# A two-way branch turned round, its target announced ahead, and the first tile's work put in another order

## The chip, the cores and the metric

The kernel runs on one core of one Trainium2 chip, in one launch. The metric is the device time of that launch in microseconds (us). The engines of a core run their own instruction streams side by side and wait for each other by semaphores: TensorE (PE, with its weight loads shown as PEld), VectorE (DVE), ScalarE (ACT), GpSimd (POOL) and SyncE (SP), which here mostly issues DMA transfers. A "q" behind an engine's name (ACTq, SPq) is its sequencer: register loads, branches, semaphore instructions and DMA issues.

## What is computed

Three stages follow each other, all in 32-bit floats, for a batch of 4 sequences of 576 tokens. The core of the reference:

```python
# 1. top-32 attention, 8 heads of 64
scores = scale * np.matmul(q, k.transpose(0, 1, 3, 2))
kth = np.partition(scores, -top_k, axis=-1)[..., -top_k:-top_k + 1]
scores = np.where(scores >= kth, scores, -1000000000.0)
attn = np.exp(scores - np.max(scores, axis=-1, keepdims=True))
attn = attn / (np.sum(attn, axis=-1, keepdims=True) + 1e-09)
x = np.matmul(attn, v)                    # -> (4, 576, 512)
# 2. one of 8 experts a token; a token whose gate is >= 0.5 keeps the expert of the token before it
fresh_e = int(np.argmax(logits[b, s]))
e = fresh_e if s == 0 or local_gate[b, s] < 0.5 else (prev_e if prev_e >= 0 else fresh_e)
p = np.exp(ls); p /= p.sum() + 1e-09      # ls: logits less their maximum
out[b, s] = p[e] * (np.maximum(x[b, s] @ w1[e], 0.0) @ w2[e])
# 3. Fourier mix over tokens and features, norm, two dense layers
mixed = np.real(np.fft.fft(np.fft.fft(x, axis=1), axis=2))
u = x + mixed
un = (u - mu) / np.sqrt(var + 1e-06)
out = u + np.maximum(un @ w_ch1, 0.0) @ w_ch2
```

## The kernel before

**Attention** works on 16 pairs of heads, 9 tiles of 128 query rows each, 144 tiles in all, in a software pipeline written out in one loop over `n`: the string `ORDER` says in which order the steps of a turn are issued, `OFF` how many tiles each step runs ahead or behind. A tile passes through four matmuls of its scores (`scores`, L452) into PSUM `acc`, their copy to SBUF `ss` (`evac_s`, ACT, L459), eight MAX8 on DVE (L465), and from there to the 32nd largest value, the mask, the softmax and the product with V. Ahead of the loop `prep_first` (L387 to L404) makes the operands of the first pair: `turn` transposes `in_k` and `in_q` on PE into `tp` (L358, and L359 for the last 64 rows); ACT and DVE then write a high part and a low part of each, for k (`kt`, L396 and L397), a copy of them to the other half of the partitions (L403, L404), and for q (`qp`, L401 and L402, 512 columns and then 64). It does so for head `s=0` and then for `s=1`, and `scores(0)` and `evac_s(0)` are issued behind all of it, though tile 0 needs head 0 alone.

**Routing** (`tokens`) runs a batch at a time. For the last batch it is a chain of small DVE, PE and ACT operations that ends in `slow_i` (L762, whether some expert has more tokens than its capacity or the fast top-32 failed) and in the copy of the token's numbers into `xtok` (L765). Five indirect DMAs on POOL (L780), each followed by a small memset (`spacer`, L786), write the batch's tokens to `xs_d` in DRAM, each at its expert's slot.

**The branch** (L1064, L1065) comes next: every engine loads `slow_i` into a register, compares, and either runs the body (exact attention again, and the tokens over an expert's capacity) or skips it. With these inputs it is skipped. The body lies in the instruction streams between the branch and what follows.

**The experts** follow. The first expert's first layer has been computed ahead of the branch for the slots that earlier batches fill (`early_layers`, PE, L605, into `acc`). Behind the branch PE transposes more tokens (L1207), ACT and DVE make the high and low parts `hh` (L1260) and `hl` (L1261) of that layer's result, and PE multiplies them with the second weights (L1281, into `m`). SP reads the index of the first expert (L1072), loads the slots that the last batch has filled (`load_slots`, `xsl<-xs_d`, L1182 and L1184; they are transposed later, at L1207 again, and multiplied at L1256), and at `j == 8` the indices of the other seven (L1379). `j` counts steps of an expert's 8 slices, `r` the experts and `f` the slices. Three tables of the Fourier stage are loaded on POOL's queue at `j == 10` and `j == 18` (L1385 to L1388).

The instructions of each engine lie in DRAM and are brought to it by DMA while it runs, in the packets of the two queues that the profile lists with the kind "instruction".

## Time and profile before

| | |
|---|---|
| median of 3 runs (lowest, highest) | 1240.64 us (1239.56, 1242.19) |
| the profiled execution | 1238.55 us |
| its span, first to last instruction | 1236.8 us |
| PE busy | 1187.6 us, 96% |
| DVE, ACT, POOL busy | 865.4, 679.0, 442.5 us |
| mean granted clock of PE | 0.987 of full speed |
| instruction DMA: q8 and q14 | 71 packets, 1.16 MB; 68 packets, 0.56 MB |

The times below count from the first instruction of the profiled execution. Attention fills the first 490 us, the experts come up to about 750 us, the Fourier mix and the dense layers take the rest. The median lies 2.09 us above the profiled execution's own time.

### The profile page before, as it was taken

To read this page: it belongs to the slowest core of one execution; us is meant where nothing else is said; L and a number is where in the kernel's file an instruction comes from. 1 tells how busy PE (TensorE), PEld (TensorE's weight loads), DVE (VectorE), ACT (ScalarE), POOL (GpSimd) and SP (SyncE) were. 2 spreads that over 40 slices of the span, in tenths; PEclk is the share of its full clock that TensorE was granted. 3 is DMA by queue.
4 is the path that set the end of the run, shared out by engine and by line. 5 is a ranking of instruction groups with operands and counts; after the bars stand their busy time and mean duration, and the time that the engine had idled before them with its cause. 6 is when DMAs were issued, how large, how long until landed. Compare 5 with 4: busy or idle time off the path is not lost.

```text
span 1236.8 us, 25334 instructions
## 1 busy us (share of the span) xinstructions
PE 1187.6 (96%) x8721; PEld 1084.6 (88%) x8721; DVE 865.4 (70%) x3598; ACT 679.0 (55%) x1440; POOL 442.5 (36%) x566
## 2 busy tenths in 40 slices
PE   6999999999999997899999999989999999999998
PEld 5999898998998996798888888979999999999997
DVE  7999899999999995476676785667744444543222
ACT  6999999999999894254445453533322222221111
POOL 3667686886777596000111112025410000000221
PEclk9999999999999998899999998999999999999999
DMA  5766635443543232686666675943310110100111
GB/s 112 209 169 193 149 81 116 127 103 84 142 101 88 69 126 99 202 265 235 209 224 209 228 254 152 243 146 125 122 50 34 35 66 6 67 1 1 52 52 52
DMA packets 124904, 154.43 MB, mean 125 GB/s; under 512 B 68007, under 2 KB 70303, under 8 KB 124668
## 3 DMA queue, kind: packets, MB, share of 16 engines
q1 hardware_dynamic: 119421, 134.81, 38.2%
q0 software_dynamic: 5200, 17.64, 4.3%
q8 instruction: 71, 1.16, 0.4%
q14 instruction: 68, 0.56, 0.1%
q10 hardware_dynamic: 144, 0.26, 0.1%
HBM read 93.03 MB, written 33.99 MB: 103 GB/s over the span
## 4 chain that ended last, share of the span: by engine, by line
PE 36%; issue 17%; POOL 2%; DVE 2%; DMA 2%; ACT 1%; another core or an unknown queue 1%; SPq 0%; POOLq 0%; ACTq 0%; DVEq 0%
PE f L1650 16%; PE f L1670 16%; POOL xf_d L961 2%; PE p L1151 1%; PE m L1539 1%; DMA raw<-xf_d 1%; PE acc L1546 1%; PE lt L1509 1%; DMA ut<-xf_d 0%; DVE wlo L230 0%; DMA xf_d<-xe,sid 0%; DVE raw L1130 0%; PE acc L1281 0%; PE m L1256 0%
## 5 line engine op out<-in xcount | busy, mean ns | idle before, releaser
L491 POOL TENSOR_TENSOR y<-ss,g 128x576 f32<-128x576 f32 x144 | 184.9, 1284 | 117.1 <-ACT g L486 66.3
L465 DVE MAX8 cd<-ss 128x8 f32<-128x72 f32 x1152 | 218.7, 221 | 9.8 <-ACT ss L459 9.1
L1654 ACT ACTIVATE fhh<-f 128x256 fp32r<-128x256 f32 x144 | 55.1, 383 | 275.9 <-PE f L1650 275.9
L1655 DVE SCALAR_TENSOR_TENSOR fhl<-f,fhh 128x256 fp32r<-128x256 f32 x144 | 61.0, 424 | 204.1 <-ACT fhh L1654 203.9
L562 PE MATMUL u<-in_v,et 128*128 128x74 f32 (+1 forms) x1600 | 184.7, 264 | 4.6 <-DVE dv L713 2.5
L562 PEld LDWEIGHTS u<-in_v,et 128*128 128x128 f32 (+1 forms) x1600 | 176.8, 181 | 9.5 <-ACT st_x L569 3.3
L545 PE MATMUL tp<-ident,z 128*128 128x128 f32 x720 | 143.4, 285 | 4.5 <-DVE lo L372 3.8
L546 PE MATMUL tp<-huge_id,bb 128*128 128x128 bf16 x720 | 132.4, 221 | 0.4 <-ACT bb L524 0.4
L452 PE MATMUL acc<-kt,qp 128*128 128x288 f32 x640 | 125.4, 324 | 6.3 <-ACT ss L459 4.0
L1681 POOL DMA_INDIRECT out_dram<-ut,orow x16 | 15.4, 963 | 308.3 <-DVE ut L1675 306.5
L486 ACT ACTIVATE g<-ss,mt 128x576 bf16<-128x576 f32 x144 | 118.3, 822 | 5.4 <-DVE mt L479 5.3
L545 PEld LDWEIGHTS tp<-ident,z 128*128 128x128 f32 x720 | 107.0, 149 | 15.4 <-POOL z L533 3.2
L524 ACT ACTIVATE bb<-ss,kth 128x576 bf16<-128x576 f32 x144 | 117.4, 815 | 0.0
L496 DVE MAX8 y<-y 128x8 f32<-128x576 f32 x144 | 107.2, 744 | 5.9 <-POOL y L491 5.9
L533 POOL TENSOR_SCALAR z<-ss,mt 128x576 f32<-128x576 f32 x144 | 108.4, 753 | 3.4 <-PE tp L546 3.4
L551 ACT ACTIVATE et<-tp 128x640 f32<-128x640 f32 x144 | 106.8, 742 | 3.5 <-PE tp L546 3.0
L961 POOL DMA_INDIRECT xf_d<-xe,sid x23 | 26.8, 1165 | 229.0 <-DVE xe L958 227.0
L459 ACT ACTIVATE ss<-acc 128x576 f32<-128x576 f32 x144 | 100.0, 694 | 12.0 <-PE acc L452 8.2
L452 PEld LDWEIGHTS acc<-kt,qp 128*128 128x128 f32 x640 | 94.5, 198 | 9.7 <-ACT ss L459 5.0
L1650 PEld LDWEIGHTS f<-nxh,whi 128*128 128x128 f32 x576 | 87.8, 188 | 14.0 <-ACT dd L1551 2.0
L230 DVE TENSOR_TENSOR wlo<-raw,whi 128x1024 fp32r<-128x1024 f32 x70 | 85.4, 1256 | 12.3 <-ACT whi L228 12.3
L1650 PE MATMUL f<-nxh,whi 128*128 128x256 f32 x576 | 91.3, 280 | 1.9 <-ACT dd L1551 1.7
(313 smaller groups left out, 2747.1 us busy)
## 6 DMA issues: line engine op xcount, KB each, us to landing
raw<-in_moe_w_dram SPq DMA_DIRECT2D x32, 1024.0 KB
kt<-hi SPq DMA_DIRECT2D x60, 144.0 KB
kt<-lo SPq DMA_DIRECT2D x60, 144.0 KB
xs_d<-xtok SPq DMA_DIRECT2D x8, 1056.0 KB
fr<-in_moe_w_ch_dram SPq DMA_DIRECT2D x16, 512.0 KB
raw<-in_moe_w_ch_dram SPq DMA_DIRECT2D x16, 512.0 KB
md<-md_d SPq DMA_DIRECT2D x9, 516.0 KB
in_k<-in_k_dram SPq DMA_DIRECT2D x32, 128.0 KB
```

Source lines behind the costliest of these rows:

```text
L452: PE.matmul(p, QP[i][:, s, o:o + 128].bitcast(F32R), KT[i][j][:, s, c].bitcast(F32R), start=(s == heads[0] and j == 0), stop=(s == heads[- ...
L465: return [lambda j=j: DVE.max(cd[:, 8 * j:8 * j + 8], SS[n][:, 72 * j:72 * j + 72]) for j in range(8)]
L486: ACT.activation(g, SS[n], AF.Sign, bias=MT[i][:, t, 1, 7:8], scale=-SCL, accum_out=DIF[n])
L491: POOL.tensor_tensor(y, SS[n], LT[n], op=OP.mult)
L496: DVE.max(y8, Y8[n])
L524: ACT.activation(t, SS[n], AF.Relu, bias=kth[:, n:n + 1], scale=-1.0)
L533: POOL.tensor_scalar(ZZ[n], SS[n], -1.0, MT[i][:, t, 0, 0:1], op0=OP.mult, op1=OP.add)
L545: PE.matmul(o, z[:, k], ident, start=True, stop=False, is_transpose=True)
L546: PE.matmul(o, bb[:, k], huge_id, start=False, stop=True)
L562: PE.matmul(p[0:m, s, 0:VW], et[:, kc, qs], vv[:, kc, VC[s]], start=(kc == 0), stop=(kc == 4))
L1650: PE.matmul(p, a[:, d, fs], x[:, d], start=(n == 0), stop=(n == 11))
L1670: PE.matmul(yp[c], a[:, c * 128:(c + 1) * 128], w[:, f, :], start=(f == 0 and n == 0), stop=(f == 3 and n == 2))
```

## The change

Four things are changed.

**The start.** Half of the first loads of k and q are issued on ACT's queue instead of SP's. `prep_first` makes head 0's operands first and calls `scores(0)` and `evac_s(0)` as soon as what they read has been issued; head 1's second copy, and the last 64 columns of q for both heads, come behind. PE gets transposes of the identity into the PSUM tile `u`, which nothing reads (`fill`): 5 ahead of the first turn, 4 behind the second, 2 behind the first scores, then 1 a turn in turns 0 and 1 and 4 in turns 2 to 5.

**The score differences** in the routing (the logits less their maximum) go to the PSUM tile `dv` instead of the SBUF tile `dl`.

**The branch.** The condition is turned round (`slow == 0`, an empty block named "fast", with the body as its Else) and the empty block is laid behind the body. An instruction that announces this block as a likely target (`hint_fast`) is put on each engine ahead of the branch: one each for PE and DVE in the routing, one for SP in turn 112, one for POOL in turn 147, and six for ACT in turns 144 to 149. The five scatters of the last batch's tokens move from ahead of the branch to behind it; the tiles they read now live in a pool that outlasts attention.

**Behind the branch.** All eight expert indices are read at once, ahead of the load of the late slots, and the three table loads move from `j == 10` and `j == 18` to the third and fourth expert.

```diff
@@ attention
+            def fill(n):
+                for _ in range(n):
+                    PE.transpose(ub[:, 0:128], ident, ident)
...
+                k_rows(0)
+                k_copies(0)
+                q_high(0, c0)
+                q_low(0, c0)
+                k_rows(1)
+                q_high(1, c0)
+                q_low(1, c0)
+                lead[0]()
+                k_copies(1)
+                lead[1]()
                 for s in range(2):
...
+                    q_high(s, c1)
+                return lambda: [q_low(s, c1) for s in range(2)]
...
-                DVE.tensor_tensor(dl, lg[:, :, 0:8], bcast(mx, [128, 5, 8]), op=OP.subtract)
+                d0 = dv[:, 136:176].rearrange("p (t e) -> p t e", t=5)
+                if last and not exact:
+                    hint_fast(EN.PE, EN.DVE)
+                DVE.tensor_tensor(d0, lg[:, :, 0:8], bcast(mx, [128, 5, 8]), op=OP.subtract)
...
-            load_pair(0, QK[::-1])
+            load_pair(0, QK[::-1], SP if exact else ACT)
...
+            def lead():
+                if not exact:
+                    scores(0)
+                    fill(2)
+
+            ends = prep_first((lead, lambda: exact or evac_s(0)))
...
+                if n < 6:
+                    fill(1 if n < 2 else 4)
...
+                if n == 112:
+                    hint_fast(EN.SP)
+                if n == 147:
+                    hint_fast(EN.Pool)
+                if 144 <= n < 150:
+                    hint_fast(EN.Activation)
@@ around the branch
+    def hint_fast(*engines):
+
+        at = list(nc.cur_bb.bb.instructions)
+        tc.mark_branch_hint_location("fast", "LikelyTaken", list(engines))
...
-    with tc.If(slow > 0):
+    with tc.If(slow == 0, label="fast", preferred_fallthrough_block=False) as cmp:
+        pass
+    with cmp.Else():
         failed = nc.values_load(fail_i[0:1, 0:1], min_val=0, max_val=1)
         with tc.If(failed > 0):
             attention(True)
+        for _ in scatter_tokens(B - 1, list(token_sc)):
+            pass
         overflow()
+    for _ in scatter_tokens(B - 1, token_sc):
+        pass
+    scat.close()
...
-    exs = [nc.values_load(exi[0:1, r:r + 1], engines=[mybir.EngineType.SP], min_val=0, max_val=E - 1) for r in range(1)]
+    exs = [nc.values_load(exi[0:1, r:r + 1], engines=[mybir.EngineType.SP], min_val=0, max_val=E - 1) for r in range(E)]
```

At the start the change shows on ACT. Its first rows before, up to the second copy of scores (`kt` and `qp` are the operands, `acc` the scores):

```order
L396 ACT_TABLE_LOAD
L396 ACTIVATE kt<-tp_149 64x576
L401 ACTIVATE qp_158<-tp_148 64x512
L401 ACTIVATE qp_158<-tp_148 64x64
L403 ACTIVATE kt<-kt 64x576
L396 ACTIVATE kt<-tp_149 64x576
L401 ACTIVATE qp_158<-tp_148 64x512
L401 ACTIVATE qp_158<-tp_148 64x64
L403 ACTIVATE kt<-kt 64x576
L459 ACTIVATE ss<-acc 128x576 x2
```

The same stretch of ACT now; line numbers are those of the changed kernel (L437 is L396 of before, L442 L403, L447 L401, L521 L459):

```order
L382 DMA in_k<-in_k_dram 128x4x64
L382 DMA in_q<-in_q_dram 128x4x64
L437 ACT_TABLE_LOAD
L437 ACTIVATE kt<-tp_159 64x576
L442 ACTIVATE kt<-kt 64x576
L447 ACTIVATE qp_167<-tp_158 64x512
L437 ACTIVATE kt<-tp_159 64x576
L447 ACTIVATE qp_167<-tp_158 64x512
L442 ACTIVATE kt<-kt 64x576
L521 ACTIVATE ss<-acc 128x576
L447 ACTIVATE qp_167<-tp_158 64x64 x2
L521 ACTIVATE ss<-acc 128x576
```

Three operations, not five, stand between ACT's first two writes and head 0's last operand and the copy of tile 0, the two short ones now come behind it, and two DMA issues stand ahead of the table load.

Around the branch it shows on POOL. Before, from the last weight split ahead of the branch to the register load of the branch's condition:

```order
L230 TENSOR_TENSOR wlo<-raw,whi 128x1024 x2
L780 DMA xs_d<-xtok,ix 18433x528
L786 MEMSET spacer 1x1
L780 DMA xs_d<-xtok,ix 18433x528
...
L780 DMA xs_d<-xtok,ix 18433x528
L786 MEMSET spacer 1x1
L1064 TENSOR_LOAD slow_i
L1065 COMPARE_AND_BRANCH
```

Now, first ahead of the branch:

```order
L1815 BRANCH_PREFETCH_HINT
L703 TENSOR_TENSOR xtok<-st_x,ri 128x4x64 x2
L703 TENSOR_TENSOR xtok<-st_x,ri 64x64 x2
L230 TENSOR_TENSOR wlo<-raw,whi 128x1024 x2
L1132 TENSOR_LOAD slow_i
L1133 COMPARE_AND_BRANCH
```

and then behind the body of the branch:

```order
L1133 UNCONDITIONAL_BRANCH
L300 DMA xs_d<-xtok,ix_147 18433x528
L306 MEMSET spacer 1x1
L300 DMA xs_d<-xtok,ix_147 18433x528
...
L300 DMA xs_d<-xtok,ix_147 18433x528
L306 MEMSET spacer 1x1
L1372 MEMSET ysb 128x4
```

The five scatters with their memsets have moved past the register load and the branch, and POOL's first memset of the experts (`ysb`) follows them directly, without the table loads.

On SP, behind the branch, before and then now:

```order
L1065 UNCONDITIONAL_BRANCH
L1072 TENSOR_LOAD exi
L1072 ISA x2
L1182 ISA
L1182 DMA xsl<-xs_d 128x528
L1182 ISA
L1182 DMA xsl<-xs_d 128x528
L1379 TENSOR_LOAD exi
```

```order
L1133 UNCONDITIONAL_BRANCH
L1147 TENSOR_LOAD exi
L1147 ISA x2
L1147 TENSOR_LOAD exi
...
L1147 TENSOR_LOAD exi
L1147 ISA x2
L1257 ISA
L1257 DMA xsl<-xs_d 128x528
```

Eight register loads instead of one now stand ahead of the loads of the late slots.

## Rows read from the trace of the kernel before

**Rows 1.** Busy time by window: engines PE, PEld, DVE, ACT, POOL, then clock, DMA share:

```profile
15.00:20.00 5.00, 4.26 (x17) 3.45 (x17) 4.34 (x30) 3.18 (x6) 0.73 (x1) 1.00 0.33 76
...
35.00:40.00 5.00, 5.00 (x48) 4.65 (x48) 4.51 (x33) 5.00 (x12) 3.05 (x3) 1.00 0.27 60
...
440.00:450.00 10.00, 9.91 (x93) 9.16 (x91) 10.00 (x69) 10.00 (x24) 9.49 (x15) 1.00 0.47 172
```

**Rows 2.** Timeline of the start: start, us, engine, what [idle before, releaser]:

```profile
3.77 0.61 SPq L351 DMA_DIRECT2D in_q<-in_q_dram  x1
4.24 1.09 PE L358 MATMUL tp<-ident,in_k 128*128 128x128 f32 x4 [4.24 <-DMA in_k<-in_k_dram]
5.66 0.64 ACT L396 ACTIVATE kt<-tp 64x576 fp32r<-64x576 f32 x1 [3.62 <-PE tp L359]
6.19 1.09 PE L358 MATMUL tp<-ident,in_q 128*128 128x128 f32 x4 [0.57 <-DMA in_q<-in_q_dram]
7.62 0.59 ACT L401 ACTIVATE qp<-tp 64x512 fp32r<-64x512 f32 x1 [1.32 <-PE tp L359]
8.24 0.68 DVE L402 SCALAR_TENSOR_TENSOR qp<-tp,qp 64x512 fp32r<-64x512 f32 x1 [1.16 <-ACT qp L401]
9.20 0.68 ACT L403 ACTIVATE kt<-kt 64x576 fp32r<-64x576 f32 x1
9.93 1.33 PE L452 MATMUL acc<-kt,qp 128*128 128x288 f32 x4 [2.35 <-ACT kt L403]
13.05 0.65 ACT L459 ACTIVATE ss<-acc 128x576 f32<-128x576 f32 x1
13.73 1.18 DVE L465 MAX8 cd<-ss 128x8 f32<-128x72 f32 x8 [0.67 <-ACT ss L459]
```

**Rows 3.** The score matmuls of the first 30 us: ns min/median/max, starts:

```profile
L452 PE MATMUL acc<-kt,qp x32: 442/442/607, 9.9 to 28.9; 128*128 128x288 f32 x32
```

**Rows 4.** The same line from 430 to 445 us:

```profile
L452 PE MATMUL acc<-kt,qp x24: 288/296/399, 429.7 to 444.3; 128*128 128x288 f32 x24
```

**Rows 5.** Timeline around the branch, columns as in Rows 2:

```profile
487.75 1.78 PE L605 MATMUL acc<-kt,whi 128*128 128x256 f32 x8
487.86 0.20 DVE L762 TENSOR_SCALAR slow_i<-tp,fail_f 1x1 int32<-1x1 f32 x1
489.11 1.06 POOL L780 DMA_INDIRECT xs_d<-xtok,ix  x1 [5.07 <-issue]
494.29 0.91 POOL L780 DMA_INDIRECT xs_d<-xtok,ix  x1 [0.23 <-issue]
496.46 1.94 PE L1207 MATMUL tp<-ident,xe 128*128 128x128 f32 x8 [6.93 <-issue]
499.18 0.96 SPq L1182 DMA_DIRECT2D xsl<-xs_d  x2
499.26 0.38 ACT L1260 ACTIVATE hh<-acc 128x256 fp32r<-128x256 f32 x1 [17.05 <-DMA xs_d<-xtok,ix]
...
513.47 0.60 PE L1207 MATMUL tp<-ident,xsl 128*128 128x128 f32 x4
```

**Rows 6.** Sequencer records of the branch's line: duration in ns, first and last start:

```profile
L1065 ACTq EVENT_SEMAPHORE  x2: 17/17/17, 491.1 to 491.2; - x2
...
L1065 PEldq EVENT_SEMAPHORE  x2: 51/51/51, 492.9 to 493.1; - x2
...
L1065 PEldq COMPARE_BRANCH  x1: 4152/4152/4152, 488.7 to 488.7; - x1
...
L1065 POOLq INC_SWDGE_SEM  x1: 587/587/587, 497.9 to 497.9; - x1
```

**Rows 7.** Windows behind the branch, columns as in Rows 1:

```profile
488.10:499.69 11.59, 3.37 (x16) 2.70 (x14) 0.29 (x3) 0.38 (x1) 5.41 (x11) 0.50 0.37 130
499.69:505.18 5.49, 5.49 (x13) 4.33 (x14) 4.98 (x8) 2.73 (x6) 1.77 (x3) 0.50 0.92 255
```

**Rows 8.** SP's reads of the seven later expert indices, columns as in Rows 6:

```profile
L1379 SPq TENSOR_LOAD <-exi x7: 262/268/281, 500.2 to 503.6; - x7
```

## The prediction

> **What bounds the kernel now.** I read the busy times by window first, to see what each stage waits for. In steady attention DVE and ACT are busy for all of 10 us, PE for 9.91 and POOL for 9.49 (the row from 440 us of [rows 1]). So a shift of the first tile, with nothing else touched, shifts the whole stage. Behind the branch PE runs without a gap once it has begun (5.49 of 5.49 [rows 7]), and it is busy for 96% of the whole span, so there too an earlier start is an earlier end. Two places remain where the bounding engines wait: the start, and the branch.

> At the start the timeline says what tile 0 waits for. DVE's first MAX8 stands at 13.73, behind ACT's copy of the scores at 13.05. The scores were done at 9.93 + 1.33 = 11.26; the copy came 1.79 us later because ACT was writing head 1's operands. The scores in turn waited for ACT's second copy of k, issued behind both parts of q [rows 2]. The first matmuls are also slow, 442 ns in the first 30 us where they take 296 later, PE at the lower of its two clocks [rows 3, 4] (the clock column prints 1.00 there; the durations decide).

> Around the branch the timeline shows the routing's last value at 487.86 + 0.20 = 488.06, PE's next matmul at 496.46 and ACT's `hh` at 499.26, and PE's full work begins at 499.69 [rows 5, 7]. The sequencer rows split this. Each engine has its condition by 488.7, but the next record comes at 491.1 on ACT and at 492.9 on PE, whose branch alone is shown with 4152 ns. PE then passes two semaphore instructions (to 493.1) and stands again until 496.46, 3.3 us. POOL comes last: five scatters from 489.11, then its own branch, and only at 497.9 + 0.59 = 498.5 does it give the semaphore step that ends the branch's line [rows 5, 6]. `hh` follows that at 499.26. So the path is scatters, POOL's branch, `hh`, second weights.

> **The change, part by part.**

> *Start.* Of the two pieces of each load that SP issues one after the other, one goes to ACT's queue; SP's issues take 0.6 us each, so k comes about 0.5 us sooner and q, behind two such issues, about 1.3 (q's tail, issued at 3.77 [rows 2], then at about 2.5). The chain with the durations of [rows 2]: k is transposed by 5.1 (4.24 + 1.09 + 0.36 for the tail, less 0.5; an estimate, like the next); q's turn follows at once and ends at 6.5. ACT: high part of k 5.15 to 5.8, its copy (0.68) to 6.5, high part of q (0.59) to 7.1; DVE's low part of q (0.68) to 7.85. Scores 7.9 to 9.25. ACT meanwhile writes head 1's two high parts and a copy (0.64 + 0.59 + 0.68 = 1.9) to 9.0, so the copy of the scores runs at 9.3 and MAX8 begins at about 9.97. Against 13.73 this is **-3.75**. Bounds: -2.5, if the loads come no earlier, and -4.5.

> *Fills.* Each is a 128-column transpose, 1.09 / 4 = 0.27 us at the low clock [rows 2]. The first 11 stand in PE's idle time. The 18 in the loop cost 18 x 0.27 = 4.9 us of PE at the low clock, and in 15 to 20 us PE has 0.74 of 5 free; if the clock rises by then, the scores of a tile take 4 x 0.15 = 0.6 us less [rows 3, 4]. DVE, the engine that bounds there, idles 0.66 of 5 from 15 us and 0.49 of 5 from 35 us [rows 1]; over the five windows of 5 us from 15 to 40, of which the first and the last are shown, 1.7 us. It can get back no more than that, and if the clock does not rise the fills put the scores off by about 1. I take about half of the gain, **-0.9**; range -1.7 to +1.

> *Score differences in PSUM.* Three operations of 40 columns change a source or target; the nearest row of such size takes 0.20 us in all [rows 5], so even a quarter of each is 0.15. I take **0**, bounds -0.15 to +0.15.

> *Branch and scatters.* POOL no longer scatters ahead of the branch, so every engine can be past it by about 489, if the hints bring the target in time, and `hh` needs no POOL any more: 489.3 and 0.38. The hint instructions themselves show in no row of before; the semaphore instructions of the same sequencers take 17 to 51 ns [rows 6], and ten hints at that are at most 0.5 us, on engines with such gaps; I take 0. What is late next is PE. Its first stand (488.7 to 492.9) goes. Its second, 3.3 us behind the exit of the skipped block, can stay: the hint names the block, not what follows it. With it: transposes 489.0 + 0.2 + 3.2 = 492.4, done at 494.35, then the second weights at 494.4 instead of 499.69, **-5.3**. Without it they begin at about 491.7 (PE's `acc` matmuls end at 489.53, the transposes take 1.94, [rows 5]), -8.0. Without a working PE hint both stands remain, 496.46 + 1.94 = 498.4: -1.3.

> *Clock behind it.* PE runs at half clock from 488.10 to 505.18, busy all of the last 5.49 us [rows 7]. With the wait 5.3 us shorter PE is sooner at full work; if the clock returns in steps like the stretches seen, some 3.9 us of full work at half clock remain, and half of the difference is saved, **-0.8**. Bounds 0 (the same 5.49) and -2.7 (no half clock at all).

> *Eight indices at once, scatters later.* Seven reads take (503.6 - 500.2) / 6 = 0.57 us each [rows 8], eight 4.6 us on SP from 489.2 to 493.8. The late slots wait for the last scatter anyway: five at a pitch of (494.29 - 489.11) / 4 = 1.3 us, from 489.8 to 496, landed by my estimate near 497.7 (`hh`, freed by the last landing and POOL, stood 4 us behind the last scatter's end), so SP issues the load near 497.8 against 499.18 [rows 5]. It comes 1.4 us earlier while PE comes 5.3 earlier. Before, PE transposes these slots only at 513.47, 14 us after the issue, so I count **0**; the indices hide under the scatters. The tables leave the crowded 499.69 to 505.18 (DMA share 0.92 [rows 7]) and are wanted after 750 us: 0.

> [...]

> *Sum.* -3.75 - 0.9 - 5.3 - 0.8 = **-10.75**. From the profiled execution's 1238.55 that is 1227.8. The median of the runs, 1240.64, lies 2.09 above this execution, so I put the changed kernel's at about **1229.5**.

> **The rivals.**

> *PE's second stand goes too.* [...] -2.7 more: 1227.

> [...]

> *The start is not carried through.* POOL is at 9.49 of 10 late in attention [rows 1] and nothing there becomes shorter; but it works tile by tile and should shift too. If half or all of the 4.65 is lost: 1232 to 1234.

> *The late slots become the wait.* With PE 5 to 8 us earlier, and its work at full clock, the slots wanted at 513.47 [rows 5] are wanted at 505 to 507; issued at 497.8 they have 7 us to land. If they need 9: +2, 1231.5.

> *Slower: the hints stop the engines.* [...] Of the ten hints, ACT's six stand in the last six turns, one a tile, and those of PE and DVE in the serial chain of routing. [...] It is slower from the point where the ten cost over 10.75 us, 1.1 each. [...] Nothing in the profile before shows such an instruction, so I can't exclude it.

> [...]

> **How the numbers follow.** Likeliest, 0.45: 1229.5. Second stand gone, 0.18: 1227. PE's hint without effect, 0.13: 1234.4. Start not carried, 0.10: 1232 to 1234. Late slots, 0.06: 1231.5. Slower, 0.06: over 1243. Nothing at all gained, 0.02. The range goes from 1224 (second stand gone and the bounds of start and clock) to 1236 (PE's hint and a start at its low bound). What this kernel's measurement can tell from no change is about 0.2%, 2.5 us: faster 0.91, same 0.03, slower 0.06.

> **What would show it.** First MAX8 near 10 and score matmuls near 296 ns by 20 us; ACT and POOL past the branch within 0.5 us of it; PE's first record behind it near 489 and its next matmul at 492.4 (relative to a branch 4.65 earlier); scatters behind the branch; the late slots' transposes without a wait. The prediction is wrong if an engine stands at a hint, if PE still resumes 4 us after its branch, or if the 4.65 us are gone at the last `slow_i`.

## The result, and the profile after

| | before | after |
|---|---|---|
| median of 5 runs (lowest, highest) | 1240.64 us (1239.34, 1243.66) | 1228.42 us (1226.70, 1231.54) |
| profiled execution, span | 1238.55, 1236.8 us | 1226.70, 1224.9 us |
| mean granted clock of PE | 0.987 | 0.993 |

The ratio is 0.9908, 95% interval [0.9891, 0.9925]: faster by about 11.4 us by the ratio, 12.2 by the medians. The prediction was 1229.5 in a range from 1224 to 1236. The profiled execution after is the fastest of its five, with the highest granted clock, so shifts read from the two profiles take in some of the clock's scatter.

The timeline of the start, after (it answers to [rows 2]; L390 is L358 of before, L437 L396, L447 L401, L514 L452, L521 L459, L527 L465):

```profile
2.68 0.61 SPq L383 DMA_DIRECT2D in_q<-in_q_dram  x1
...
3.84 1.11 PE L390 MATMUL tp<-ident,in_k 128*128 128x128 f32 x4 [1.09 <-DMA in_k<-in_k_dram]
...
5.27 1.08 PE L390 MATMUL tp<-ident,in_q 128*128 128x128 f32 x4
5.29 0.64 ACT L437 ACTIVATE kt<-tp 64x576 fp32r<-64x576 f32 x1 [2.11 <-PE tp L391]
...
6.69 0.59 ACT L447 ACTIVATE qp<-tp 64x512 fp32r<-64x512 f32 x1
...
8.05 1.33 PE L514 MATMUL acc<-kt,qp 128*128 128x288 f32 x4 [0.35 <-DVE qp L451]
...
9.41 0.65 ACT L521 ACTIVATE ss<-acc 128x576 f32<-128x576 f32 x1
...
10.09 1.18 DVE L527 MAX8 cd<-ss 128x8 f32<-128x72 f32 x8
...
13.87 1.09 PE L390 MATMUL tp<-ident,in_k 128*128 128x128 f32 x4 [2.22 <-DMA in_k<-in_k_dram]
15.18 1.33 PE L514 MATMUL acc<-kt,qp 128*128 128x288 f32 x4
...
16.55 0.65 ACT L521 ACTIVATE ss<-acc 128x576 f32<-128x576 f32 x1 [0.61 <-PE acc L514]
...
20.12 0.77 PE L514 MATMUL acc<-kt,qp 128*128 128x288 f32 x4
```

Up to the first MAX8 (10.09, forecast 9.97) all is as worked out. Then something new: at 13.87 PE transposes the second pair's k, for whose DMA it has waited 2.22 us, and tile 2's scores (15.18) stand behind it in PE's queue. By 20 us four score matmuls take 0.77 us instead of 1.33: PE is at the higher of the two levels that these times show.

Before, the same transposes stood in the same place, without a wait for the load:

```profile
14.89 1.09 PE L358 MATMUL tp<-ident,in_k 128*128 128x128 f32 x4
...
17.57 0.65 ACT L459 ACTIVATE ss<-acc 128x576 f32<-128x576 f32 x1 [0.61 <-PE acc L452]
```

So tile 2 comes earlier only by as much as this k does, 1.02 us.

Around the branch, after (to [rows 5]; L825 is L762, L1335 L1260, L1282 L1207, L300 L780, L1356 L1281, L1257 L1182):

```profile
484.38 0.20 DVE L825 TENSOR_SCALAR slow_i<-tp,fail_f 1x1 int32<-1x1 f32 x1
...
486.62 0.38 ACT L1335 ACTIVATE hh<-acc 128x256 fp32r<-128x256 f32 x1 [7.80 <-PEq L1133]
486.90 1.94 PE L1282 MATMUL tp<-ident,xe 128*128 128x128 f32 x8 [0.56 <-PEq L1133]
...
487.94 1.06 POOL L300 DMA_INDIRECT xs_d<-xtok,ix  x1 [7.94 <-DVE hl L1336]
...
488.50 1.20 PE L1356 MATMUL m<-whi,hh 128*128 128x512 f32 x2
...
496.75 0.95 SPq L1257 DMA_DIRECT2D xsl<-xs_d  x2
...
501.00 0.60 PE L1282 MATMUL tp<-ident,xsl 128*128 128x128 f32 x4
```

The sequencer records of the branch, after (to [rows 6]):

```profile
L1133 ACTq EVENT_SEMAPHORE  x2: 17/17/17, 485.6 to 485.7; - x2
...
L1133 PEldq EVENT_SEMAPHORE  x2: 51/51/51, 486.4 to 486.5; - x2
...
L1133 PEldq COMPARE_BRANCH  x1: 388/388/388, 485.2 to 485.2; - x1
...
L1133 POOLq INC_SWDGE_SEM  x1: 496/496/496, 486.2 to 486.2; - x1
```

From the start of its branch ACT takes 0.48 us to the next record (2.47 before), PE 1.17 (4.21 before), and PE passes the exit to its transposes in 0.4 us where it stood 3.3. The announcements show with the line of the program's end, and take 31 to 65 ns each:

```profile
L1815 ACTq BRANCH_PREFETCH_HINT  x6: 31/31/50, 459.1 to 470.1; - x6
...
L1815 PEldq BRANCH_PREFETCH_HINT  x1: 45/45/45, 471.2 to 471.2; - x1
```

Windows behind the branch, after (to [rows 7], same columns):

```profile
485.05:488.50 3.45, 2.89 (x16) 2.63 (x14) 0.85 (x2) 1.18 (x3) 0.56 (x1) 0.50 0.07 14
488.50:491.13 2.63, 2.63 (x8) 2.12 (x7) 2.31 (x3) 2.01 (x4) 2.20 (x5) 0.50 0.39 153
491.13:497.00 5.87, 5.87 (x38) 5.27 (x37) 4.70 (x7) 1.72 (x3) 3.31 (x7) 1.00 0.40 140
```

PE works 2.63 us at the lower clock behind the start of the second weights, against 5.49 before.

Where the time went, from start times in the two profiled executions:

| | before | after | shift |
|---|---|---|---|
| copy of tile 0's scores | 13.05 | 9.41 | -3.64 |
| copy of tile 2's scores | 17.57 | 16.55 | -1.02 |
| MAX8 of the mask step, tile 14 | 64.13 | 61.41 | -2.72 |
| the routing's last value | 487.86 | 484.38 | -3.48 |
| first second weights | 499.69 | 488.50 | -11.19 |
| transposes of the late slots | 513.47 | 501.00 | -12.47 |
| end of the span | 1236.8 | 1224.9 | -11.9 |

The row of tile 14 depends on the execution of the old start that one compares with. In the profile of before, PE is at the lower clock until 34 us. before_d0, described below, has the same start and no fills, and there it is at the higher clock from 26 us on, and tile 14 stands 1.63 us earlier. First before, then before_d0:

```profile
28.07 1.31 PE L452 MATMUL acc<-kt,qp 128*128 128x288 f32 x4
...
64.13 0.74 DVE L496 MAX8 y<-y 128x8 f32<-128x576 f32 x1
```

```profile
27.43 0.79 PE L452 MATMUL acc<-kt,qp 128*128 128x288 f32 x4
...
62.50 0.74 DVE L496 MAX8 y<-y 128x8 f32<-128x576 f32 x1
```

Between tile 14 and the routing lies one thing that the change doesn't touch: before, PE was at the lower clock from 402.8 to 406.2 us, and after it was not (1.00 throughout 395 to 410). It is worth some 1.2 us here (the shift of the mask step's MAX8 is -2.60 at tile 110 and -3.79 at the last tile), and nine of the twelve profiles below, with the new start and with the old, have such a stretch near 400 us.

### The profile page after: what moved, and what is told of

Read it like the earlier page. It is cut to its first block, busy times and chain, and to the rows that moved or that the text cites. A ratio compares the mean times of both kernels' runs of the same rounds, so it can differ in the third digit from the quotient of the medians.

```text
span 1224.9 us, 25380 instructions
## 1 busy us (share of the span) xinstructions
PE 1186.5 (97%) x8750; PEld 1082.3 (88%) x8750; DVE 867.2 (71%) x3598; ACT 680.3 (56%) x1440; POOL 445.0 (36%) x566
## 4 chain that ended last, share of the span: by engine, by line
PE 36%; issue 17%; POOL 3%; DMA 2%; DVE 1%; ACT 0%; SPq 0%; POOLq 0%; DVEq 0%; ACTq 0%
PE f L1723 16%; PE f L1743 16%; POOL xf_d L1028 2%; PE p L1226 1%; PE acc L1356 1%; DMA ut<-xf_d 1%; DMA md_d<-dd 1%; PE m L1331 1%; PE lt L1582 1%; POOL xs_d L300 0%; DMA xf_d<-xe,sid 0%; PE m L1612 0%; PE acc L1619 0%; DVE wlo L230 0%; POOL md L1547 0%
## 5 line engine op out<-in xcount | busy, mean ns | idle before, releaser
L527 DVE MAX8 cd<-ss 128x8 f32<-128x72 f32 x1152 | 218.6, 221 | 8.5 <-ACT ss L521 7.8
L514 PE MATMUL acc<-kt,qp 128*128 128x288 f32 x640 | 122.9, 319 | 1.6 <-ACT ss L521 1.2
L521 ACT ACTIVATE ss<-acc 128x576 f32<-128x576 f32 x144 | 99.9, 694 | 9.8 <-PE acc L514 6.1
L514 PEld LDWEIGHTS acc<-kt,qp 128*128 128x128 f32 x640 | 91.9, 193 | 4.9 <-ACT ss L521 2.3
L230 DVE TENSOR_TENSOR wlo<-raw,whi 128x1024 fp32r<-128x1024 f32 x70 | 85.4, 1257 | 12.4 <-ACT whi L228 12.3
```

The costliest lines, as they stand in the source:

```text
L514: PE.matmul(p, QP[i][:, s, o:o + 128].bitcast(F32R), KT[i][j][:, s, c].bitcast(F32R), start=(s == heads[0] and j == 0), stop=(s == heads[- ...
L527: return [lambda j=j: DVE.max(cd[:, 8 * j:8 * j + 8], SS[n][:, 72 * j:72 * j + 72]) for j in range(8)]
```

## The experiments

Each was timed against the kernel before on its own chip; a gain in us is (1 - ratio) times that chip's median of before (1240.2 to 1241.2). "Behind" is the time from the start of the routing's last value to that of the first second weights in the profile: 11.83 before, 4.12 after. The intervals are some 2 us to either side, up to 3 for the kernels with few runs, so a difference of two gains is uncertain by about 3 us; what an engine does in one profile is read from its rows.

| run | ratio, 95% interval | gain, us | behind, us |
|---|---|---|---|
| start_only | 1.0010 [0.9994, 1.0026] | -1.2 | 10.2 |
| start_d0 | 0.9963 [0.9943, 0.9983] | 4.6 | 10.09 |
| before_d0 | 1.0004 [0.9986, 1.0021] | -0.5 | 12.2 |
| after_dl | 0.9951 [0.9933, 0.9969] | 6.1 | 4.12 |
| branch_only | 0.9964 [0.9950, 0.9978] | 4.5 | 6.47 |
| branch_hint146 | 0.9935 [0.9912, 0.9958] | 8.1 | 6.73 |
| no_hints | 0.9946 [0.9926, 0.9967] | 6.7 | 7.00 |
| scat_ahead | 0.9932 [0.9911, 0.9952] | 8.4 | 7.87 |
| after_pad | 0.9924 [0.9903, 0.9944] | 9.4 | 3.74 |
| before_pad_small | 0.9996 [0.9979, 1.0013] | 0.5 | 11.82 |
| k1_first | 0.9868 [0.9843, 0.9893] | 16.4 | 3.75 |
| k1_nofill_hint | 0.9916 [0.9893, 0.9938] | 10.4 | 6.45 |

### The start alone, and the score differences

**start_only** is the changed kernel with everything but the start undone, except that the tiles stay in the pools of the changed kernel.

```diff
-                d0 = dv[:, 136:176].rearrange("p (t e) -> p t e", t=5)
+                d0 = dl
...
-    with tc.If(slow == 0, label="fast", preferred_fallthrough_block=False) as cmp:
+    with tc.If(slow > 0):
```

Expected: 

> Only the start is changed; branch, scatters, indices, tables and score differences are as before. Theory A (the prediction's): the first tile comes 3.75 us earlier, the fills add 0.9, all of it is carried: 4.65 us faster than the kernel before. Theory B (from the trace of the changed kernel): most of the 3.64 us of the first tile is lost at tile 2, where PE waits for the second pair's k (tile shift -1.0), the faster clock gives back to -2.7 by tile 14, and the rest is the clock drop near 403 us that may or may not come: 2.5 to 3.8 us faster, with a wait for in_k at about 14 us in the trace.

Both theories fell: no gain at all. The trace has the copy of tile 0 3.50 us ahead of before and tile 110 2.2 ahead, and then the routing's last value 2.8 behind it (490.64). The timeline of that stretch names one operation:

```profile
476.51 5.08 DVE L743 TENSOR_SCALAR dl<-dl 128x40 f32<-128x40 f32 x1
476.90 4.64 POOL L230 TENSOR_TENSOR wlo<-raw,whi 128x1024 fp32r<-128x1024 f32 x2
```

In the changed kernel the same operation reads PSUM:

```profile
475.25 0.20 DVE L745 TENSOR_SCALAR dl<-dv 128x40 f32<-128x40 f32 x1 [0.27 <-ACT pr L739]
475.33 4.67 POOL L230 TENSOR_TENSOR wlo<-raw,whi 128x1024 fp32r<-128x1024 f32 x2
```

With both operands in SBUF it ends at 481.59, as POOL's second split ends (481.54); from PSUM it takes 0.20 us beside the same splits. So in this trace the operation stands while POOL works, and for longer than one operation of POOL: it begins 0.39 us ahead of the first split, beside the third of POOL's four multiplications, and outlasts both splits. Yet the kernel before has it at 0.19 us beside the second of these multiplications, so that work of POOL beside it is not enough to make it stand; what is, the traces do not show. First before, then start_only:

```profile
478.27 0.62 POOL L643 TENSOR_TENSOR xtok<-st_x,ri 128x256 f32<-128x256 f32 x1
478.74 0.19 DVE L682 TENSOR_SCALAR dl<-dl 128x40 f32<-128x40 f32 x1
```

```profile
476.40 0.28 POOL L703 TENSOR_TENSOR xtok<-st_x,ri 64x64 f32<-64x64 f32 x1
```

Three kernels tell what the edit is worth. **before_d0** is the kernel before with this edit alone, **after_dl** the changed kernel with `d0 = dl` alone, **start_d0** is start_only with the first line of its diff left as it was.

Expected: 

> The kernel before with one edit: the score differences go to PSUM. Theory Z (the prediction's): worth nothing, within 0.15 us. Theory L (from the run with the start alone, where DVE's operation on the score differences, SBUF to SBUF, took 5.08 us until POOL's two weight splits had ended, and 0.19 in the profiled execution of before): DVE has to wait for POOL's running operations when both operands are in SBUF, and not when it reads PSUM; executions in which it meets the splits lose 4.9 us. If it meets them in a third to a half of the executions of before, this is 1.5 to 2.5 us faster on the whole, and its spread of times is smaller.

Expected: 

> The changed kernel with the score differences back in SBUF. Theory Z: no change, 12.2 us faster than before. Theory L: the operation stands behind POOL's splits in most executions, since the changed start brings POOL and DVE there as in the run with the start alone: up to 4.9 us slower than the changed kernel, 7.3 to 10 faster than before, and the operation of some 5 us shows in the profile.

Expected: 

> The start and the score differences in PSUM; branch, scatters, indices and tables as before. The run with the start alone was no faster than before, though its first 470 us were 2.2 us ahead. Theory L: with the 5 us wait gone, the 2.2 us reach the end: 2 to 3.5 us faster than before, 5 faster than the start alone. Theory Z, with the loss elsewhere: as slow as the start alone.

In the kernel before the edit is worth nothing that can be measured, as predicted; the interval leaves at most 1.7 us of the 1.5 to 2.5 that theory L gave it there. In the changed kernel it is worth 11.4 - 6.1 = 5.3 us (the two intervals do not overlap), and after_dl's profile has the operation with 5.08 us again (480.79). With the start it decides between -1.2 and +4.6. So it gains nothing by itself and keeps off a loss which the rest of the change would bring. What of the rest brings it is not shown: in start_only POOL's multiplications ahead of the splits are released one DVE operation sooner than before (by `ri` instead of `ltt`), which puts DVE's operation 1.3 us behind their start instead of 1.05, beside the third of them instead of the second.

start_d0 also shows a part that I had not priced. Its branch is the old one, yet the second weights come 10.09 behind instead of 11.83, since ACT's first result is released by POOL's branch and no longer by the scatters' landing (in [rows 5]: `xs_d`):

```profile
495.27 0.38 ACT L1318 ACTIVATE hh<-acc 128x256 fp32r<-128x256 f32 x1 [15.68 <-POOLq L1122]
```

The scatters' sources lie in a pool of their own there, as in the changed kernel, so that most likely what follows attention no longer has to wait for them. By the two profiles that is 1.7 of its 4.6 us, and it belongs to the branch, not to the start.

### The branch alone

**branch_only** is the changed kernel with the start of before.

```diff
-            ends = prep_first((lead, lambda: exact or evac_s(0)))
+            prep_first()
...
-                if n < 6:
-                    fill(1 if n < 2 else 4)
```

Expected: 

> The changed kernel with the start of before (loads on one queue, old order, no fills). Theory A: the branch part is worth 5.3 + 0.8 = 6.1 us, so 6.1 faster than before. Theory B (trace of the changed kernel): 7.7 us between the routing's last value and the second weights, and about 1.3 at the low clock behind it, less some 0.6 lost later: 8.4 to 9 us faster than before. If the parts don't interact, this and the run with the start alone add up to the 12.2 us of the whole change.

4.5 us, less than either theory, and with start_d0's 4.6 the parts fall some 2 us short of the whole, which is within the noise of three ratios. The branch's line has a reason all the same:

```profile
L1098 PEldq COMPARE_BRANCH  x1: 3464/3464/3464, 487.5 to 487.5; - x1
```

PE stands at the branch though it has its announcement; the second weights come 6.47 us behind instead of 4.12. Without the 29 fills, of two instructions each, PE's branch lies 58 instructions earlier in its stream. In the changed kernel one packet of queue q8 is fetched between announcement and branch (477.4), here none. By its times q8 most likely carries PE's instructions: from 1001 to 1100.2 us of before, five of its packets go with 1293 matmuls and weight loads. **branch_hint146** is branch_only with the announcement moved ahead of the last fetch, for the case that it needs one behind it.

```diff
-                    hint_fast(EN.PE, EN.DVE)
+                    hint_fast(EN.DVE)
...
+                if n == 146:
+                    hint_fast(EN.PE)
```

Expected: 

> The changed kernel with the start of before, and PE's announcement moved 178 instructions ahead, to turn 146. In the run with the start of before PE stood 3.46 us at the branch although it had its announcement 140 instructions ahead; without the 29 fills its branch lies 58 instructions earlier in the stream, and between announcement and branch no packet of instructions was fetched. [...] Rival: the announcement is lost with the distance, or the start was what counted; no change, 4.5 faster than before.

```profile
L1100 PEldq COMPARE_BRANCH  x1: 3720/3720/3720, 487.4 to 487.4; - x1
```

PE stands as before, 3.72 us against 3.46, though here a packet of q8 (468.4) is fetched between announcement (463.9) and branch (487.4): such a packet by itself does not make the announcement act. (The gain of 8.1 is not the branch's: "behind" is 6.73, no shorter than branch_only's. Its interval overlaps with branch_only's, and its profile lacks the stretches at the lower clock that branch_only's has at 401.5, 794.0 and 817.9 us.) In the profiles where PE's announcement acts (after, after_pad, after_dl, scat_ahead, k1_first) PE stands 0.38 to 0.39 us and its branch lies 58 instructions later in its stream than in the three where it doesn't. So the place of the branch seems to decide. No run moved the branch by itself, so this is argued and not shown, and the rule stays open.

### Announcements and scatters

**no_hints** is the changed kernel with all calls of `hint_fast` left out.

```diff
-                    hint_fast(EN.PE, EN.DVE)
...
-                if n == 112:
-                    hint_fast(EN.SP)
-                if n == 147:
-                    hint_fast(EN.Pool)
-                if 144 <= n < 150:
-                    hint_fast(EN.Activation)
```

Expected: 

> The changed kernel without any of the ten announcements; branch turned round and scatters behind it as in the changed kernel. Theory A: every engine stands 2.5 to 4.2 us at the branch as before, PE is the last (4.15 us less the 1.2 that it still takes with the announcement), 3.0 us slower than the changed kernel, 9.2 faster than before. Theory R (the announcements do little, and taking POOL's scatters off the path gives the gain): within 1 us of the changed kernel.

```profile
L1125 PEldq COMPARE_BRANCH  x1: 3868/3868/3868, 486.6 to 486.6; - x1
```

Theory A held: "behind" grows by 2.9 us, the time by 4.7 (the difference of two ratios, each uncertain by 2 to 2.6 us). PE is not alone here: ACT, DVE, POOL and SP each stand 3 to 4.2 us too. PE has no second stand here:

```profile
L1125 PEldq EVENT_SEMAPHORE  x2: 51/51/51, 490.6 to 490.7; - x2
...
491.21 1.94 PE L1274 MATMUL tp<-ident,xe 128*128 128x128 f32 x8 [3.44 <-SPq L1125]
```

It goes on 0.5 us behind the exit. So in the changed kernel it is not the announcement that takes the second stand away.

**scat_ahead** puts the five scatters back ahead of the branch and keeps the announcements.

```diff
-                if last:
-                    token_sc.extend(prev_sc)
-                    return
...
-    for _ in scatter_tokens(B - 1, token_sc):
-        pass
```

Expected: 

> The changed kernel with the five scatters ahead of the branch again, announcements and all else as changed. Theory A: ACT's first result waits for POOL again; POOL reaches the branch 6.4 us later (five at 1.3), passes it in 1.5 us with its announcement: the second weights come about 9.5 us behind the routing's last value instead of 4.1: 5 us slower than the changed kernel, 7 faster than before. Rival R (the announcements give the gain alone): within 1 us of the changed kernel.

```profile
496.72 0.38 ACT L1328 ACTIVATE hh<-acc 128x256 fp32r<-128x256 f32 x1 [12.54 <-POOLq L1130]
```

ACT waits for POOL again, as expected; "behind" grows by 3.8 us instead of 5.4, because ACT is released by POOL's passing the branch and not by the landing. PE's transposes are done meanwhile. The time fits, with 3.0 us less gained, but the intervals of the two ratios overlap: against rival R it is the row that decides.

### PE's second stand

**after_pad** and **before_pad_small** add instructions inside the body of the branch, which is not run. The diff shows the first, which is otherwise the changed kernel; before_pad_small is the kernel before with 16 instead of 89, and with the change's moves of the expert indices and of the tables.

```diff
+                    for d in (89 if f == 0 else 0) * [0]:
+                        PE.transpose(p[:, 0:128], xo[:, 0:128], ident)
```

Expected: 

> [...] Theory H (the announcement removed both stands, wherever the block lies): no change, 12.2 us faster than before.

Expected: 

> The kernel before with 16 transposes (32 instructions of PE) added inside the body of the branch, which is not run, and with the two small moves of the change: all eight indices read at once behind the branch, tables loaded at the third and fourth expert. Theory P (PE's second stand comes from where the target lies in its stream: the two runs with the old branch but 58 more instructions ahead of it pass the same exit without it): PE goes on within 0.3 us of the exit, its transposes come about 3 us sooner. The time stays as before in any case, since ACT's first result still waits for POOL 5 us later, and if the small moves are hidden as predicted: within 2 us of before. Rival H (the exit itself costs 3 us): the second stand is still there.

after_pad shows no second stand, as theory H has it: "behind" is 3.74, and PE passes the exit as after. Its 89 transposes, 178 instructions of PE, move the target on in PE's stream, and this alone does not bring the stand back, here, where the target was announced. Its gain of 9.4 us, with nothing that runs changed, against the changed kernel's 11.4 shows what two kernels can differ by without a cause. before_pad_small did what theory P said:

```profile
L1067 PEldq EVENT_SEMAPHORE  x2: 51/51/51, 490.7 to 490.9; - x2
...
L1067 PEldq COMPARE_BRANCH  x1: 3672/3672/3672, 487.0 to 487.0; - x1
```

```profile
491.24 1.94 PE L1209 MATMUL tp<-ident,xe 128*128 128x128 f32 x8 [3.17 <-PEq L1067]
```

PE still stands at the branch itself, but goes on 0.3 us behind the exit, where [rows 5, 6] have 3.3 us. start_only and start_d0, with the old branch and no announcement, pass the exit without it too (0.7 and 0.4 us), and before_d0, with the target where before has it, shows it (exit at 493.0, transposes at 496.17). So the exit costs nothing by itself; in these five runs, without an announcement, the second stand hangs on where the target lies in PE's stream. Why it does is not shown. The time of before_pad_small is that of before, since POOL was the last there: a stand off the path cost nothing that can be measured, and the two small moves neither.

### A version that takes the new wait away

**k1_first** loads the second pair's k ahead of its q, and the constant tables behind both.

```diff
-            if not exact:
-                load_consts()
...
-            load_pair(1, QK)
+            load_pair(1, QK[::-1])
+            if not exact:
+                load_consts()
```

Expected: 

> The changed kernel with the second pair's k loaded ahead of its q, and both ahead of the constant tables on SP's queue. Theory W: in the changed kernel 2.6 us of the start are lost where PE waits for this k at 13.9 us with tile 2's scores queued behind; k then lands by about 9 us, and tile 2's copy is 3.6 us ahead of before instead of 1.0. What remains by tile 14 is less, since the clock comes back by 20 us and DVE has had 2.7 already: 0.5 to 1.5 us faster than the changed kernel (13 to 14 faster than before). Rival: the pipeline behind is bound by DVE from tile 5 on and has the 2.7 either way; no change.

```profile
5.44 0.96 SPq L382 DMA_DIRECT2D in_k<-in_k_dram  x2
...
11.59 1.06 PE L390 MATMUL tp<-ident,in_k 128*128 128x128 f32 x4
...
14.24 0.65 ACT L521 ACTIVATE ss<-acc 128x576 f32<-128x576 f32 x1 [0.60 <-PE acc L514]
```

PE no longer waits for k; tile 2's copy stands at 14.24 instead of 16.55, the routing's last value at 482.21 instead of 484.38. Its median is 1222.92, the ratio to before 0.9868: 16.4 us faster, 5 more than the change, and more than theory W gave (the intervals of the two ratios just overlap). By the two profiles 2.2 us of the 5 are there at the routing's last value, and neither has a stretch at the lower clock on the way; in its profile PE is also back at the higher clock at 485.8, before its second weights, and not at 491.1.

**k1_nofill_hint** is this version without the 29 fills and with PE's announcement as in branch_hint146.

```diff
-                if n < 6:
-                    fill(1 if n < 2 else 4)
...
+                if n == 146:
+                    hint_fast(EN.PE)
```

Expected: 

> The version with the second pair's k loaded first, without any of the 29 fills, and with PE's announcement at turn 146 (so that it still acts). Theory F (the fills bring the clock back some 6 us sooner, which the engines that bound the first tiles keep): 1 to 2 us slower than with the fills, the clock at full only from about 26 us instead of 18. Rival G (the fills only moved the branch in PE's stream): as fast as with them, 17 to 18 us faster than before on the same chip.

It is 6 us slower than with the fills, and its profile shows three reasons that the time can't part: the mask step's MAX8 of tile 14 is 1.7 us later (60.77 against 59.08, theory F; PE falls back to the lower clock from 25.2 to 32.0), PE stands 3.4 us at the branch again, since the announcement doesn't act here either ("behind" 6.45 against 3.75), and PE was at the lower clock from 400.7 to 410.9, which k1_first was not. So in this pair of profiles the fills do both, and theory G's half, 2.7 us, is the larger. The third reason shows in profiles with the fills too (scat_ahead, from 399.8 to 413.4).

## Why the prediction was right, point by point

The time was right, within 1.1 us, and the two places were the right ones. Its own sum, 1240.64 - 10.75, gives 1229.9 and not 1229.5. That the total came out so close is partly luck: of the start 2.7 us less was carried than forecast, the branch gave 2.4 more, and some 1.2 of the clock near 400 us was in no term.

- **Start, -3.75, carried.** The first tile gained 3.64. The step that failed is that all of it is carried: 2.6 us of it went into a new wait two tiles on, for the second pair's k, behind which tile 2's scores stood in PE's queue. I had followed the first pair's loads through SP's queue and not the next pair's, which stand behind the constants. k1_first shows it by taking the wait away.
- **Fills, -0.9.** 1.7 us from tile 2 to tile 14 in the two profiles of the result, and the same 1.7 between k1_nofill_hint and k1_first; that is the whole of the bound I had set. But the five profiled kernels with the old start and no fills differ by as much among themselves: tile 14's MAX8 stands at 62.50 (before_d0), 62.51 (branch_only), 64.01 (before_pad_small), 64.13 (before) and 64.19 (branch_hint146). Measured from each one's own tile 2 the fills are worth 0.0 to 0.2 us against the first two and 1.7 to 1.8 against the others, 1.1 in the mean, so -0.9 is not refuted. In all eight profiles with fills PE is at the higher clock by 18 to 22 us and stays there past 140; without them it gets there at 26 or 34 us, or falls back for 7 us. Start and fills together are 2.7 by tile 14 instead of 4.65; another 1.2 by the clock near 400 us is not the change's.
- **Score differences, 0.** Right against before (before_d0), wrong as a part of this change, which without it gains 6.1 (after_dl). I costed the operation by its own duration and did not ask which engine it might have to wait for.
- **Branch, -5.3; measured -7.7.** POOL's scatters came off the path and the first stands went, as forecast. The step that failed is "Its second, 3.3 us behind the exit of the skipped block, can stay: the hint names the block, not what follows it." It went, as the rival with 0.18 said. before_pad_small shows that it came from the target's place and not from the exit, and no_hints that at the changed kernel's place it is gone without an announcement. What the traces have of it: before, one packet of q8 moves in each of PE's two stands (489.7 and 493.8), after, one as PE passes the exit (486.5). For the case that the second stand goes, the prediction had the second weights at 491.7, 3.8 behind the last value's start, and the trace has 4.12.
- **Clock behind the branch, -0.8.** 1.3 (from 11.19 to 12.47). The forecast put 3.9 us of full work at the lower clock, a figure that it works out from no row; the trace has 2.63.
- **Indices, late slots, tables, 0.** The late slots are issued at 496.75, 12.4 behind the last value where 9.9 were forecast (POOL began its scatters only at 487.94), and transposed at 501.00 without a wait all the same; before_pad_small finds no difference in the two moves.
- **The rivals.** No engine stood at an announcement (31 to 65 ns each), so no run shows what the 0.06 for slower rests on. PE's announcement without effect is what branch_only and k1_nofill_hint have: 2.35 and 2.7 us more "behind" than after and than k1_first, smaller than the forecast 4. The 1234.4 for it counts both stands of PE; no run with announcements shows both. The forecast let an announced PE pass the branch in 0.2 us and an unannounced one in 4.2; the trace has 1.2 with the announcement, and 3.5 in these two where it has no effect.

From the late slots (12.5 us) the shift grows to 13.0 at 773 us and falls to 11.7 by 812 us, in the Fourier stage; this wasn't followed up.

## What to carry to other kernels

When the first piece of a pipeline is brought forward, follow the queue that feeds the second and third as well: the load that was early enough before is the next wait. A branch whose body is hardly ever run costs each engine 2.5 to 4.2 us here where its target is not announced, so engines should pass it before their long work and not behind it, and what was wanted only by one consumer behind it (here five scatters) should not stand ahead of it. A change of some 60 instructions far away went with 2 to 3 us more at the branch, most likely because it moved the branch in its stream: look at the branch's own record after every edit. And before a gain is put down to an edit, compare several profiles of the code without it: here they differ by 1.7 us at tile 14 through the clock alone.
